# Reordering a linear-attention and channel-mix kernel: earlier loads of batches 1 and 2, and batch 3's gate input on GpSimd

## The chip, the cores and the metric

One core of a Trainium2 chip runs the whole program. The metric is device time in microseconds, taken over whole executions; the profile comes from one further execution. The engines are named as in the profile: PE is TensorE (PEld its weight loads), DVE is VectorE, ACT is ScalarE, POOL is GpSimd, and SP issues most of the DMAs.

## The reference

Two layers in a row, for 4 batches of 1088 positions. The first is attention with a polynomial sketch, 4 heads of 32:

```
phi(x) = outer(S1 x, S2 x)              # 8 x 8 = 64 features per position
kv = sum over s of phi(k) v^T           # 64 x 32 per head
z  = sum over s of phi(k)
x  = (phi(q) kv) / (phi(q) z + 1e-6)    # heads side by side: 128 per position
```

The second is a channel mix on x, with the position before it:

```
xk = mu_k x + (1 - mu_k) x_prev ;  xr = mu_r x + (1 - mu_r) x_prev
v  = relu(xk w_k)^2 w_v                 # 128 -> 1024 -> 128
out = sigmoid(xr w_r) * v
```

The output is 4 x 1088 x 128 in float32.

## The kernel before, in words

Everything fits on the chip at once. The positions of a batch are cut into 32 stretches of U = 34 units; with 4 heads that makes 128 partitions, so a batch of k or q is one [128, 34*32] tile. The kernel is written as small functions, each of which issues the instructions of one task, and one string, `ORDER`, lists all tasks in the order in which they are issued. Each engine works through its own tasks strictly in the order of the string; semaphores make it wait for what a task reads or overwrites. An entry such as `kp.2.0.G^an.1.2.V@...` is task kp of batch 2, half 0, on GpSimd (A is ScalarE, V VectorE, P VectorE with one operand from PSUM), tied behind the VectorE task an.1.2 by an added wait; the digits behind @ are the PSUM banks. There are 8 banks of 512 float32 columns.

The tasks of one batch b of the attention, in the order of their data:

- `turn.k`, `turn.q` (lines 261, 264): VectorE transposes k and q in blocks of 32. Batches in `WHOLE_K` are transposed in two instructions, so that four units lie side by side.
- `kproj` (274 or 280): S1 k and S2 k on TensorE into PSUM, in two halves. With the batch in `WHOLE_K` a half is 4 or 5 matmuls of 128 columns (line 274), otherwise four times as many on tiles of 32 columns (line 280). `abev` copies the halves to SBUF.
- `kp` (298): the outer products, phi(k), in two halves, on GpSimd or VectorE. `kvmm` (327) sums phi(k) v^T on TensorE, `kvev`, `kvt`, `kvtev` copy and transpose it.
- `zmm` (307), `zev`, `wmm` (315), `wsq` (318): z, folded with S into a small matrix SQ.
- `abw` (365, 369, 381, 386): S1 q, S2 q and q's product with z, on TensorE; `abwev` evacuates. `pw`, `den` (413, 414), `an` (422): the denominator, its reciprocal, and one factor divided by it. `qp` (431): the outer products phi(q).
- `qd` (440) or, for batch 0, `qt`, `qtt`: phi(q) transposed, on VectorE or TensorE. `xmm` (513, 496), `xt`, `xev`, `xtev`, `xs`: x on TensorE and its evacuation, with a shift for x_prev. `TURN = "ODDD"` says that batch 0 goes by TensorE and the others by VectorE; `WHOLE_Q` is read only where TURN is "O".

The channel mix works in nine groups g: two of 512 columns for each batch (g = 2b, 2b+1) and one, g = 8, of 256 for the last two units of all batches. `xk` (529) and `xkt` mix for w_k, `xh` and `xht` copy x in bf16 for the gate. Then per group, in four pieces: `f1` (553) = w_k times xk, `relu` (561) on ScalarE, `sq` (574, 576) on any engine, `f2` (586) into one bank. `rr` (599) is the gate's matmul, `sig` (607) the sigmoid, `fin` (612) the product, `st` (622, 618) the stores, two halves for each group. `cset` prepares small constants; `wset` converts the weights to bf16 (0 is w_k, 1 is w_v, 2 is w_r). `zz` (175) are matmuls on zeros into an otherwise free place.

The loads are issued ahead of all that, as `LOADS` lists them: S1 and S2, mu, k, q and v of each batch, weights w0 (w_k), w1 (w_v), w2 (w_r). All but three small ones go through SP's queue. A DMA's semaphore is used again by the eighth DMA after it, so that SP issues a load only when the one eight before it has landed.

Of the kernel before, what the change touches and what calls it, by code (L numbers as in the profile page):

```python
# [50 lines left out]
qp.2.0.V sq.3.1.V xh.1.0.G^sq.3.1.V kvev.2.V qp.2.1.G abwev.3.1.V kvev.3.V kvt.2 relu.3.2.A f1.3.0@45 relu.3.0.A
pw.3.2.G qd.2.0.V qd.2.1.V f1.3.3@01 relu.3.3.A kvtev.2.V sq.3.0.V f2.1.0@2 f2.1.1 kvt.3 kvtev.3.A f1.2.3@34
relu.2.3.A sq.2.3.V xh.1.1.G f2.1.2 den.3.2 f1.2.2@01 relu.2.2.A f2.1.3 sq.3.2.A xmm.2.2@3456 xev.2.0.A
sq.2.1.G^sq.2.3.V xt.2@0 fin.1 st.1.0.S st.1.1.S rr.2@1 xtev.2.V xs.2.G xh.2.0.G an.3.2.G f2.3.0@7 xev.2.1.V sq.2.2.A
sig.2.A xk.2.0 xkt.2 xk.2.1 qp.3.0.V f2.2.0@2 qd.3.0.V f2.3.1 f2.2.1 f1.4.0@01 f2.2.2 f1.4.1@34 sq.3.3.A relu.4.0.A
f2.2.3 fin.2 st.2.0.S st.2.1.S relu.4.1.A f1.4.3@56 relu.4.3.A qp.3.1.G^qp.3.0.V sq.4.0.G rr.3@0 sig.3.A f1.5.3@34
f2.3.2 f2.3.3 f1.4.2@56 qd.3.1.V relu.5.3.A fin.3 st.3.0.S st.3.1.S sq.4.3.V relu.4.2.A sq.4.2.V f1.5.0@12 sq.4.1.V
rr.4@0 sig.4.A xt.3@3 xh.2.1.V xtev.3.A sq.5.3.V xs.3.V relu.5.0.A sq.5.0.G^xs.3.V xmm.3.2@4567 f2.4.0@0 xev.3.0.A
xev.3.1.A xkt.3 f1.5.1@12 f2.4.1 f2.4.2 xk.3.0 xk.3.1 rr.5@3 xht.3.V relu.5.1.A sig.5.A f1.5.2@12 sq.5.1.V f2.4.3
xh.3.0.V relu.5.2.A sq.5.2.V f1.6.3@45 relu.6.3.A fin.4 st.4.0.S st.4.1.S xh.3.1.V f2.5.0@3 f1.6.0@67 f2.5.1 sq.6.3.V  # L60
# [13 lines left out]
def kernel(  # L74
# [51 lines left out]
    UH = {"k": {"": (0, U), "0": (0, 18), "1": (18, U)}, "q": {"": (0, U), "0": (0, 16), "1": (16, U)}}  # L126

    def load(what, eng):
        e = nc.sync if eng == "S" else nc.scalar if eng == "A" else nc.gpsimd
        x, b, i = what[0], int(what[1]), what[2:]  # L130
        if x == "S":
            e.dma_start(S16[R * b:R * b + R, :], S2 if b else S1)
        elif x == "m":
            e.dma_start(mu_row[b:b + 1, :], (moe_mu_r if b else moe_mu_k).rearrange("d -> () d"))
        elif x in "kq":
            src = (k if x == "k" else q)[b].rearrange("h (a u) d -> (h a) (u d)", u=U)
            lo, hi = UH[x][i]
            for lo, hi in ((lo, hi),) if i else ((0, U // 2), (U // 2, U)):
                e.dma_start((kin if x == "k" else qin)[b][:, lo * D:hi * D], src[:, lo * D:hi * D])
# [17 lines left out]
    nc.vector.memset(warm[:], 0.0)  # L157
# [94 lines left out]
    def turn(x, b, y, eng="V"):  # L252
        lo, hi = UH[x][str(y) if y < 2 else ""]
        t, src = (kT, kin) if x == "k" else (qT, qin)
        t = t[b % 2][:].rearrange("p u a -> p (u a)")
        if x == "k" and b in WHOLE_K:

            for c in (0, 2):
                u, n = CU[c]
                if lo <= u < hi:  # L260
                    nc.vector.transpose(_ap(t, [[32, 2], [P, n], [1, 32]], 32 * c),
                                        src[b][:, D * u:D * (u + 2 * n)].rearrange("p (c m d) -> p c m d", c=2, m=n))
        else:
            nc.vector.transpose(t[:, 32 * lo:32 * hi], src[b][:, D * lo:D * hi])  # L264
# [3 lines left out]
    def kproj(b, j, banks):  # L268
# [3 lines left out]
        for m in range(m0, m1):  # L272
            if b in WHOLE_K:
                nc.tensor.matmul(_ap(o[:, 32 * (m - m0):], [[n, 2], [1, 32]]),  # L274
# [402 lines left out]
```

## Time and profile before

| | us |
|---|---|
| median of 3 runs | 81.2 (81.06 to 81.69) |
| the profiled execution | 81.55 |
| its span, first to last instruction | 79.8 |
| first f1 matmul starts | 22.8 |
| last TensorE work ends | 75.35 |

The span is cut by the profile into windows, groups of like instructions and a chain of waits, the sequence of work that ended last. A row of a group gives line, engine, operation, tiles out<-in, shape, count, then busy us, the mean ns of one, and the idle time of the engine just before with what ended it. A row of the timeline begins with start and duration in us; a row of the chain likewise, with what the chain spent that stretch on. Neighbouring instructions of a kind are merged into one row (x16 is 16 of them). A TensorE matmul's own duration holds its latency, so that for TensorE the chain's pieces tell more than the means.

### The profile page before, as it was taken

How to read it: one execution, taken by the hardware profiler on the slowest of the kernel's cores; microseconds unless marked ns; L12 is line 12 of the kernel's file. 1: busy time of each engine (PE TensorE's matmuls, PEld its weight loads, DVE VectorE, ACT ScalarE, POOL GpSimd, SP SyncE). 2: the span in 40 equal slices, each digit the busy share in tenths (PEclk: the TensorE clock that was granted, in tenths of full speed). 3: DMA queues.
4: the chain of work that ended last, by engine and by line, in shares of the span. 5: the costliest groups of instructions: out<-in, count | busy, mean ns of one | idle time of the engine just before them, and what ended most of it. 6: DMA issues, size and time to landing. Idle time of an engine off the chain costs nothing.

```text
span 79.8 us, 3602 instructions
## 1 busy us (share of the span) xinstructions
PE 73.0 (91%) x1558; PEld 54.1 (68%) x1558; DVE 64.0 (80%) x121; ACT 58.5 (73%) x87; POOL 43.2 (54%) x55
## 2 busy tenths in 40 slices
...
GB/s 1 268 281 227 253 360 341 192 227 314 397 403 248 205 151 83 8 0 8 0 105 36 11 0 0 8 133 11 5 136 126 4 0 72 125 74 0 80 246 7
DMA packets 9876, 10.26 MB, mean 129 GB/s; under 512 B 1122, under 2 KB 7268, under 8 KB 9860
## 3 DMA queue, kind: packets, MB, share of 16 engines
...
q0 software_dynamic: 64, 0.13, 0.7%
q10 hardware_dynamic: 308, 0.13, 0.6%
...
HBM read 7.80 MB, written 2.23 MB: 126 GB/s over the span
## 4 chain that ended last, share of the span: by engine, by line
PE 83%; DMA 7%; issue 2%; SPq 1%; DVE 1%; DVEq 0%
PE ps L586 19%; PE ps L553 19%; DMA qx<-in_q_dram 7%; PE ps L327 6%; PE ps L513 6%; PE ps L386 5%; PE ps L599 5%; PE ps L274 5%; PE ps L175 3%; PE ps L369 2%; PE ps L451 2%; PE ps L479 1%; PE ps L307 1%; PE ps L496 1%; PE ps L280 1%
## 5 line engine op out<-in xcount | busy, mean ns | idle before, releaser
L561 ACT ACTIVATE k<-ps 128x1024 bf16<-128x1024 f32 (+1 forms) x36 | 33.3, 1010 | 0.6 <-PE ps L553 0.6
L586 PEld LDWEIGHTS <-k 128*128 128x128 bf16 x272 | 16.9, 98 | 4.1 <-issue 0.4
L586 PE MATMUL ps<-wv,k 128*128 128x128 bf16 x272 | 19.1, 219 | 0.0
L553 PE MATMUL ps<-xk,wk 128*128 128x512 bf16 x64 | 17.6, 379 | 0.0
L576 DVE TENSOR_TENSOR k<-k 128x1024 bf16<-128x1024 bf16 (+1 forms) x23 | 14.2, 648 | 0.9 <-ACT k L561 0.9
L431 POOL TENSOR_TENSOR qp<-an,abw 128x1024 f32<-128x1024 f32 (+1 forms) x5 | 10.2, 2047 | 1.7 <-DVE qp L431 1.7
L298 POOL TENSOR_TENSOR kp<-ab 128x1024 f32<-128x1024 f32 (+1 forms) x5 | 10.6, 2134 | 0.0
L576 POOL TENSOR_TENSOR k<-k 128x1024 bf16<-128x1024 bf16 x4 | 7.6, 1893 | 5.3 <-DVE qx L204 3.0
L574 ACT ACTIVATE k<-k 128x1024 bf16<-128x1024 bf16 x9 | 9.6, 1073 | 0.0
L175 PE MATMUL ps<-zero 128*128 128x512 bf16 x22 | 8.1, 489 | 1.0 <-DVE warm L157 1.0
L553 PEld LDWEIGHTS <-wk 128*128 128x128 bf16 x72 | 6.0, 100 | 2.6 <-DVE XT L532 0.3
L440 DVE STREAM_TRANSPOSE qpT<-qp 128x1152 f32<-128x1152 f32 (+1 forms) x6 | 7.6, 1294 | 0.1
L264 DVE STREAM_TRANSPOSE qT<-qx 128x1088 f32<-128x1088 f32 (+2 forms) x5 | 5.3, 1068 | 1.9 <-DMA qx<-in_q_dram 1.9
L622 POOL DMA_DIRECT2D out_dram<-k x2 | 1.3, 663 | 9.8 <-DVE k L612 9.8
L202 ACT COPY ab<-ps 128x320 f32<-128x320 f32 (+1 forms) x5 | 2.1, 419 | 5.5 <-PE ps L280 2.9
L529 DVE SCALAR_TENSOR_TENSOR xk<-ps,rat,qx 128x512 bf16<-128x512 f32 x8 | 5.7, 746 | 0.5 <-ACT qx L202 0.5
L607 ACT ACTIVATE k<-ps 128x512 f32<-128x512 f32 x8 | 5.2, 644 | 0.6 <-PE ps L599 0.6
L612 DVE TENSOR_TENSOR k<-ps,k 128x512 f32<-128x512 f32 x8 | 5.3, 668 | 0.1
L513 PE MATMUL ps<-qpT,kvt 32*32 32x256 f32 x192 | 5.2, 385 | 0.1
L327 PEld LDWEIGHTS ps<-kp,v 128*32 128x32 f32 x288 | 4.3, 110 | 1.3 <-issue 0.4
L327 PE MATMUL ps<-kp,v 128*32 128x64 f32 x288 | 4.9, 220 | 0.1
L386 PE MATMUL ps<-SQ,qT 128*32 128x96 f32 x192 | 5.0, 247 | 0.0
...
## 6 DMA issues: line engine op xcount, KB each, us to landing
out_dram<-k SPq DMA_DIRECT2D x28, 64.0 KB, 1.7
k<-in_k_dram SPq DMA_DIRECT2D x6, 272.0 KB, 6.9
qx<-in_q_dram SPq DMA_DIRECT2D x6, 272.0 KB, 6.3
...
```

The lines of the kernel that those rows point to most:

```text
L175: nc.tensor.matmul(PS[:, banks[0], :], zero[:], _ap(zero[:], [[0, 4], [1, P]]), skip_group_check=True)
L298: e.tensor_mul(o[:], _ap(a_, list(a_.ap[1:]) + [[0, R]]), _ap(b_, [list(b_.ap[1]), [0, R], list(b_.ap[2])]))
L327: nc.tensor.matmul(o[32 * h:32 * h + 32, :], vin[b][:, h, m, :], sb["kp", b, j][:, 4 * (m - KG[j][0]) + h].rearrange("p i j -> p (i j)"), ...
L386: nc.tensor.matmul(d, qT[b % 2][:, 16 * g + (quad(t) + c if TURN[b] == "O" else 4 * c + t), :], SQ[b][:], skip_group_check=True, tile_posi ...
L431: e.tensor_mul(o[:, :s1 - s0], _ap(a_, list(a_.ap[1:]) + [[0, R]]), _ap(b_, [list(b_.ap[1]), [0, R], list(b_.ap[2])]))
L440: nc.vector.transpose(sb["qpT", b][:].rearrange("p s y a -> p (s y a)")[:, F * s0:F * s1], sb["qp", b, g][:].rearrange("p s i j -> p (s i ...
L513: nc.tensor.matmul(o[32 * h:32 * h + 32, c, :], sb["kvt", b][y, f, 32 * h:32 * h + 32], m, start=(f == 0), stop=(f == 1), skip_group_check ...
L553: nc.tensor.matmul(h[:, c, :], wk[:, 2 * cp + c].rearrange("p y f -> p (y f)"), x, skip_group_check=True)
L561: nc.scalar.activation(o[:, :, :size(g)], h, RELU)
L574: nc.scalar.activation(o[:, :, :n], k1[:, :, :n], SQUARE)
L576: (nc.gpsimd if eng == "G" else nc.vector).tensor_mul(o[:, :, :n], k1[:, :, :n], k1[:, :, :n])
L586: nc.tensor.matmul(o[:, i * P:i * P + P], k2[:, c, i * P:i * P + P], wv[:, 2 * cp + c, :], start=(cp == 0 and c == 0 and i == 0), stop=(cp ...
```

## The change

- `WHOLE_K` gets batch 3. `WHOLE_Q` loses batches 1 and 2.
- `LOADS`: the two halves of k1 go ahead of v0; k2 and q2 go ahead of v1, w2 and w1. The halves now have names of their own ("a" and "b", 17 units each) and are cut where they were cut before.
- Loads of v on ScalarE's queue, were there any, would be issued behind the first activation. There are none.
- `ORDER` is another order of the same tasks. zz goes from 17 matmuls in the string to 9 (5 further ones ahead of the string stay). Among the tasks that change engine: abev.0.0 from VectorE to ScalarE, cset.4 from GpSimd to ScalarE, kp.0.1, kp.1.0 and kp.2.0 from VectorE to GpSimd, kp.3.0 the other way, qp.0.0 and qp.1.0 from GpSimd to VectorE, qp.2.0 and qp.3.0 the other way; sq on VectorE 0.1, 1.2, 1.3, 2.0, 2.1, 2.2, 3.2, 5.0 in place of 1.0, 1.1, 2.3, 3.0, 3.1, 8.3; xh.3.0 and xh.3.1 from VectorE to GpSimd; the last store, st.8.0, from SP to ScalarE, and st.6.0 from SP to GpSimd in place of st.6.1. New ties: kp.1.0 behind an.0.0, kp.2.0 behind an.1.2, wset.0 behind cset.3, and some others.

```diff
-WHOLE_K = (1, 2)
-WHOLE_Q = (0, 1, 2)
+WHOLE_K = (1, 2, 3)
+WHOLE_Q = (0,)
 LOADS = """
-S0@A S1@S m0@A m1@A k00@S k01@S q01@S q00@S v00@S v01@S v02@S v03@S k1@S q1@S w0@S v10@S v11@S v12@S v13@S w2@S w1@S
-k2@S q2@S k3@S q3@S v20@S v21@S v22@S v23@S v30@S v31@S v32@S v33@S
+S0@A S1@S m0@A m1@A k00@S k01@S q01@S q00@S k1a@S k1b@S v00@S v01@S v02@S v03@S q1a@S q1b@S w0@S k2a@S k2b@S q2a@S
+q2b@S v10@S v11@S v12@S v13@S w2@S w1@S k3a@S k3b@S q3a@S q3b@S v20@S v21@S v22@S v23@S v30@S v31@S v32@S v33@S
 """
 ORDER = """
-turn.k.0.0.V smm.0@0 cset.0 turn.k.0.1.V zz.5@7 kproj.0.1@0 abev.0.1.A kproj.0.0@1 turn.q.0.1.V cset.4.G abev.0.0.V
-smm.1@2 cset.1.V cset.2.G turn.q.0.0.V kp.0.0.G zz.1@7 zmm.0@3 zev.0.A zz.2@7 wmm.0 wsq.0 kp.0.1.P zz.2@7 abw.0.0@2
-abwev.0.0.A pw.0.0.P den.0.0 an.0.0.V abw.0.1@3 abwev.0.1.A pw.0.1.G^an.0.0.V kvmm.0@2 kvev.0.A zz.2@7 kvt.0
-turn.k.1.2.V zz.3@7 kproj.1.1@0 den.0.1 qp.0.0.G an.0.1.G qp.0.1.P abev.1.1.A kp.1.1.G kproj.1.0@1 abev.1.0.A
-kvtev.0.A qt.0.0@45 qtev.0.0.A turn.q.1.2.V wset.0.G qtt.0@2 qt.0.1@67 qttev.0.A zmm.1@3 zev.1.A qtev.0.1.A zz.2@5
-wmm.1 xmm.0.0@45 xt.0 xtev.0.A xev.0.0.A xmm.0.1@67 kp.1.0.P xev.0.1.A wsq.1 abw.1.1@3 cset.3 xs.0.V xk.0.0 xh.0.0.A
-xk.0.1 xh.0.1.A abw.1.0@1 abwev.1.1.V xkt.0 abwev.1.0.A f1.0.3@45 wset.2.G^xs.0.V relu.0.3.A f1.0.0@67 wset.1.G
-relu.0.0.A pw.1.2.G f1.1.3@23 f1.1.2@01 rr.0@4 sig.0.A relu.1.2.A relu.1.3.A turn.k.2.2.V kproj.2.1@5 den.1.2
-kproj.2.0@6 abev.2.0.A turn.q.2.2.V f1.1.0@01 kvmm.1@4 abev.2.1.V zmm.2@2 turn.k.3.2.V kproj.3.0@3 kp.2.0.P
-kproj.3.1@5 relu.1.0.A zev.2.A wmm.2 f1.0.1@01 sq.0.0.A kvev.1.A kvt.1 abev.3.1.V abev.3.0.A sq.0.3.G relu.0.1.A wsq.2
-f1.0.2@67 relu.0.2.A abw.2.0@3 an.1.2.G qp.1.0.G qp.1.1.G kvtev.1.A rr.1@0 qd.1.0.V qd.1.1.V sig.1.A sq.0.1.A
-abwev.2.0.V abw.2.1@1 abwev.2.1.A xmm.1.2@4567 turn.q.3.2.V kp.3.1.G zmm.3@3 xt.1@1 xev.1.1.V sq.0.2.A xtev.1.V
-kp.3.0.G zev.3.V f2.0.0@0 f2.0.1 xev.1.0.A wmm.3 xs.1.G sq.1.2.A f2.0.2 sq.1.3.A xkt.1 f2.0.3 xk.1.0 pw.2.2.G xk.1.1
...
-st.5.1.S sq.6.1.V sq.6.2.V f1.7.0@01 relu.7.0.A sq.7.0.V f2.6.0@2 xht.1.V sq.7.1.V f1.8.0@45 relu.8.0.A rr.7@3 f2.6.1
-f1.7.3@67 relu.7.3.A sq.7.3.V sq.8.0.V f2.6.2 f1.7.2@01 relu.7.2.A f2.6.3 sq.7.2.V f1.8.1@45 relu.8.1.A rr.6@6 sig.6.A
-f2.7.0@7 f1.8.3@01 relu.8.3.A f2.7.1 sq.8.1.V f1.8.2@45 relu.8.2.A f2.7.2 sig.7.A f2.7.3 xht.2.G rr.8@0 fin.6 st.6.0.S
-st.6.1.G sq.8.3.V sig.8.A sq.8.2.V f2.8.0@4 f2.8.1 fin.7 st.7.0.S st.7.1.A f2.8.2 f2.8.3 fin.8 st.8.0.S
+smm.0@0 turn.k.0.0.V cset.0 turn.k.0.1.V zz.5@7 kproj.0.0@0 turn.q.0.1.V abev.0.0.A kproj.0.1@1 kp.0.0.G abev.0.1.A
+kp.0.1.G smm.1@2 cset.1.V cset.4.A zmm.0@1 zev.0.A zz.2@7 wmm.0 wsq.0 zz.2@7 abw.0.1@2 abwev.0.1.A turn.q.0.0.V
+abw.0.0@1 abwev.0.0.A turn.k.1.2.V kproj.1.0@0 abev.1.0.A kvmm.0@3 kvev.0.A kproj.1.1@0 abev.1.1.A cset.2.G pw.0.1.P
+den.0.1 an.0.1.G pw.0.0.P den.0.0 an.0.0.V qp.0.0.P qp.0.1.P qtt.0@4 qttev.0.V kvt.0 kvtev.0.V qt.0.0@56 qtev.0.0.A
+zmm.1@0 zev.1.A turn.q.1.2.V qt.0.1@12 wmm.1 wsq.1 cset.3 xt.0 turn.k.2.2.V qtev.0.1.A kp.1.0.G^an.0.0.V xmm.0.0@56
+xev.0.0.A xtev.0.A xs.0.A xk.0.0 xh.0.0.A kp.1.1.G abw.1.1@0 xmm.0.1@12 xev.0.1.A abwev.1.1.A xkt.0 turn.q.2.2.V
+abw.1.0@3 abwev.1.0.A wset.0.G^cset.3 pw.1.2.G xk.0.1 f1.0.0@56 wset.2.G kproj.2.1@4 relu.0.0.A kproj.2.0@0 abev.2.1.A
+f1.1.0@45 den.1.2 xh.0.1.G an.1.2.V f1.0.2@67 sq.0.0.A abev.2.0.A zmm.2@0 relu.1.0.A kp.2.0.G^an.1.2.V zev.2.A
+qp.1.0.P kvmm.1@1 kvev.1.V f1.0.1@45 qp.1.1.G turn.k.3.2.V wmm.2 relu.0.2.A relu.0.1.A f1.0.3@23 relu.0.3.A kvt.1
+kvtev.1.A rr.0@6 f1.1.1@45 relu.1.1.A kproj.3.1@7 abev.3.1.A qd.1.0.V wsq.2 f1.1.2@23 relu.1.2.A sq.0.2.A abw.2.1@0
+abwev.2.1.A qd.1.1.V abw.2.0@7 kp.2.1.G turn.q.3.2.V abwev.2.0.V sq.0.1.V sq.0.3.A wset.1.G xmm.1.2@1234 xev.1.1.A
+pw.2.2.V xev.1.0.A xt.1@0 xtev.1.V den.2.2 xkt.1 kproj.3.0@7 abev.3.0.A sig.0.A sq.1.0.A xs.1.G^pw.2.2.V xk.1.0 xk.1.1
+kvmm.2@5 zmm.3@0 sq.1.1.A zev.3.V sq.1.2.V f2.0.0@6 f1.2.0@12 relu.2.0.A f2.0.1 kp.3.1.G an.2.2.V qp.2.0.G^an.2.2.V
+xh.1.0.G f1.2.3@34 f2.0.2 kp.3.0.P wmm.3 wsq.3 relu.2.3.A sq.2.3.A f2.0.3 f1.1.3@12 relu.1.3.A qp.2.1.G f2.1.0@0
+abw.3.1@3 abw.3.0@4 fin.0 qd.2.0.V kvev.2.A st.0.1.S abwev.3.1.A f1.2.1@67 relu.2.1.A abwev.3.0.V sq.2.0.V qd.2.1.V
+sq.1.3.V kvt.2 kvtev.2.A sq.2.1.V f1.2.2@12 relu.2.2.A f1.3.0@34 relu.3.0.A sq.2.2.V st.0.0.S f2.1.1 f1.3.1@67 f2.1.2
+rr.1@5 sig.1.A pw.3.2.G^sq.2.0.V den.3.2 xh.1.1.G^sq.2.2.V f2.1.3 fin.1 st.1.0.S an.3.2.G relu.3.1.A xmm.2.2@1234
+xev.2.1.A xt.2@5 f1.3.2@67 xtev.2.V xs.2.A kvmm.3@0 xev.2.0.V xk.2.0 qp.3.0.G qp.3.1.G xkt.2 relu.3.2.A f1.3.3@67
...
+sq.4.1.V sq.5.3.V sq.6.3.V f2.5.0@6 f1.7.2@45 f2.5.1 sq.4.2.V relu.7.2.A sq.6.0.V f1.6.2@01 relu.6.2.A xht.1.V f2.5.2
+sq.6.2.V f1.4.3@23 relu.4.3.A st.2.1.S f2.4.0@7 xh.2.1.G sq.7.2.V f2.5.3 f1.7.0@45 sq.4.3.V f2.4.1 relu.7.0.A
+f1.6.1@01 xht.2.V sq.7.0.V f2.4.2 relu.6.1.A sq.6.1.V st.3.1.S rr.4@2 sig.4.A f1.7.1@34 relu.7.1.A f2.6.0@5 f2.4.3
+rr.5@2 sig.5.A f2.6.1 f1.7.3@01 f1.8.1@34 xh.3.0.G relu.7.3.A f2.6.2 rr.6@2 f2.6.3 fin.4 st.4.0.S f1.8.0@01 fin.5
+st.5.0.S sq.7.1.V relu.8.1.A sig.6.A st.5.1.S sq.7.3.V f1.8.2@67 relu.8.2.A relu.8.0.A fin.6 st.6.1.S sq.8.0.V
+f2.7.0@3 xh.3.1.G^sq.6.1.V rr.7@4 f2.7.1 f1.8.3@67 f2.7.2 f2.7.3 sq.8.1.V f2.8.0@5 st.4.1.S sig.7.A rr.8@4 relu.8.3.A
+sq.8.3.A sq.8.2.V sig.8.A fin.7 st.7.1.A st.7.0.S st.6.0.G f2.8.1 f2.8.2 f2.8.3 fin.8 st.8.0.A
 """
...
-            for lo, hi in ((lo, hi),) if i else ((0, U // 2), (U // 2, U)):
-                e.dma_start((kin if x == "k" else qin)[b][:, lo * D:hi * D], src[:, lo * D:hi * D])
+            e.dma_start((kin if x == "k" else qin)[b][:, lo * D:hi * D], src[:, lo * D:hi * D])
...
-    for entry in LOADS.split():
-        load(*entry.split("@"))
-    nc.scalar.activation(warm[:], warm[:], SIGMOID)
+
+    for late in (0, 1):
+        for entry in LOADS.split():
+            if late == (entry[0] == "v" and entry.endswith("A")):
+                load(*entry.split("@"))
+        if not late:
+            nc.scalar.activation(warm[:], warm[:], SIGMOID)
```

More of the change, by code (lines that the diff above doesn't have):

```diff
@@ L46 @@
-f1.0.2@67 relu.0.2.A abw.2.0@3 an.1.2.G qp.1.0.G qp.1.1.G kvtev.1.A rr.1@0 qd.1.0.V qd.1.1.V sig.1.A sq.0.1.A
-abwev.2.0.V abw.2.1@1 abwev.2.1.A xmm.1.2@4567 turn.q.3.2.V kp.3.1.G zmm.3@3 xt.1@1 xev.1.1.V sq.0.2.A xtev.1.V
-kp.3.0.G zev.3.V f2.0.0@0 f2.0.1 xev.1.0.A wmm.3 xs.1.G sq.1.2.A f2.0.2 sq.1.3.A xkt.1 f2.0.3 xk.1.0 pw.2.2.G xk.1.1
-f1.1.1@12 relu.1.1.A f1.2.0@45 relu.2.0.A wsq.3 fin.0 st.0.0.S st.0.1.S f1.3.1@67 den.2.2 sq.1.1.V an.2.2.V abw.3.0@0
-abw.3.1@1 relu.3.1.A f1.3.2@23 f1.2.1@45 sq.2.0.A sq.1.0.V relu.2.1.A xht.0.G kp.2.1.G kvmm.2@6 kvmm.3@7 abwev.3.0.A
@@ L51 @@
[L51 to L60, printed above, removed]
@@ L61 @@
-relu.6.0.A f1.6.1@12 relu.6.1.A f2.5.2 f1.6.2@45 relu.6.2.A f2.5.3 f1.7.1@67 relu.7.1.A sq.6.0.V fin.5 st.5.0.S
-st.5.1.S sq.6.1.V sq.6.2.V f1.7.0@01 relu.7.0.A sq.7.0.V f2.6.0@2 xht.1.V sq.7.1.V f1.8.0@45 relu.8.0.A rr.7@3 f2.6.1
-f1.7.3@67 relu.7.3.A sq.7.3.V sq.8.0.V f2.6.2 f1.7.2@01 relu.7.2.A f2.6.3 sq.7.2.V f1.8.1@45 relu.8.1.A rr.6@6 sig.6.A
-f2.7.0@7 f1.8.3@01 relu.8.3.A f2.7.1 sq.8.1.V f1.8.2@45 relu.8.2.A f2.7.2 sig.7.A f2.7.3 xht.2.G rr.8@0 fin.6 st.6.0.S
-st.6.1.G sq.8.3.V sig.8.A sq.8.2.V f2.8.0@4 f2.8.1 fin.7 st.7.0.S st.7.1.A f2.8.2 f2.8.3 fin.8 st.8.0.S
+smm.0@0 turn.k.0.0.V cset.0 turn.k.0.1.V zz.5@7 kproj.0.0@0 turn.q.0.1.V abev.0.0.A kproj.0.1@1 kp.0.0.G abev.0.1.A
```

8 lines of the change are left out of this document (7 added, 1 removed).

## The prediction

> **What bounds the kernel now.** I read the page's head and its chain first, then busy time before and after the first f1 matmul, then the chain piece by piece, then the timeline of the first 22 us.
>
> ```profile
> span 79.8 us, 3602 instructions
> PE 73.0 (91%) x1558; PEld 54.1 (68%) x1558; DVE 64.0 (80%) x121; ACT 58.5 (73%) x87; POOL 43.2 (54%) x55
> PE 83%; DMA 7%; issue 2%; SPq 1%; DVE 1%; DVEq 0%
> PE ps L586 19%; PE ps L553 19%; DMA qx<-in_q_dram 7%; PE ps L327 6%; PE ps L513 6%; PE ps L386 5%; PE ps L599 5%; PE ps L274 5%; PE ps L175 3%; PE ps L369 2%; PE ps L451 2%; PE ps L479 1%; PE ps L307 1%; PE ps L496 1%; PE ps L280 1%
> core 0: us, PE busy (x) PEld busy (x) DVE busy (x) ACT busy (x) POOL busy (x), PEclk, DMA share, GB/s
> 8.70:22.86 14.16, 14.05 (x300) 11.12 (x301) 10.75 (x23) 6.76 (x16) 11.56 (x12) 1.00 1.06 306
> 22.86:75.40 52.54, 52.26 (x1164) 39.94 (x1164) 48.60 (x84) 49.91 (x69) 29.64 (x26) 1.00 0.26 69
> ```
>
> The chain is 83% TensorE. From 22.86 us, where the first f1 begins, to 75.40 TensorE is busy 52.26 of 52.54 us: 0.28 us of idle time is all that a better order could fill there, with ScalarE (49.91) close behind. That stretch can start earlier or hold less TensorE work, and little else. Ahead of it TensorE looks busy too, but the chain's 3% on L175, 2.4 us, are the zz matmuls, filler that computes nothing. So the first stage has slack, and its length is set on VectorE and GpSimd.
>
> ```profile
> 2.07 5.41 DMA qx<-in_q_dram
> 14.45 0.65 PE ps L175 x3
> 22.86 1.84 PE ps L553 x8
> 25.14 2.02 PE ps L274 x18
> 28.86 1.04 PE ps L280 x70
> 75.44 0.42 DVE rt L612
> ```
>
> **Part 1: an earlier zmm.0.**
>
> ```profile
> 5.58 1.23 PE L280 MATMUL ps<-SK,kT 128*32 128x64 f32 x72
> 8.20 0.45 DVE L204 COPY ab<-ps 128x320 f32<-128x320 f32 x1
> 8.71 0.38 PE L307 MATMUL ps<-ab 128*32 128x32 f32 x18 [1.04 <-DVE ab L204]
> L204 POOL COPY SQ<-SK 128x64 f32<-128x64 f32 x4 | 0.8, 233 | 3.2 <-DVE SK L215 3.2
> ```
>
> Before, abev.0.0 stands behind turn.q.0.1 on VectorE, which waits for q01 until 7.48 (2.07 + 5.41), so zmm.0 starts at 8.71. After, both evacuations are ScalarE's, behind a kproj.0 that ends at 6.81: done near 7.3, and zmm.0 goes at 7.4. It does not carry through: wmm.0 needs cset.1, which stays behind turn.q.0.1, and cset.4's four copies now stand ahead of zev.0 on ScalarE (0.8 us, by what GpSimd took). Worth by itself: nothing, because of part 2.
>
> **Part 2: k1 ahead of v0, and a new VectorE order.**
>
> ```profile
> 8.84 0.33 SPq L139 DMA_DIRECT2D qx<-in_q_dram  x1
> k<-in_k_dram SPq DMA_DIRECT2D x6, 272.0 KB, 6.9
> GB/s 1 268 281 227 253 360 341 192 227 314 397 403 248 205 151 83 8 0 8 0 105 36 11 0 0 8 133 11 5 136 126 4 0 72 125 74 0 80 246 7
> 12.12 0.31 DVE L406 TENSOR_TENSOR pw<-abw,ps 128x144 f32<-128x144 f32 x1 [0.99 <-ACT abw L202]
> 13.19 0.31 DVE L422 TENSOR_TENSOR an<-abw,den 128x144 f32<-128x144 f32 x1
> 13.41 1.36 DVE L261 STREAM_TRANSPOSE kT<-k 128x576 f32<-128x576 f32 x2
> 18.51 2.18 POOL L210 TENSOR_SCALAR wk<-wk_f,omu 128x1024 bf16<-128x1024 f32 x1
> L431 DVE TENSOR_TENSOR qp<-an,abw 128x1152 f32<-128x1152 f32 x2 | 2.7, 1349 | 0.0
> L264 DVE STREAM_TRANSPOSE qT<-qx 128x1088 f32<-128x1088 f32 x3 | 3.8, 1283 | 0.0
> ```
>
> SP's issue of q1's second half at 8.84 had waited for q00 to land. k1 is then next: two transfers of 272 KB. At 253 to 360 GB/s (slices 8 to 12 us) 557 kB take 1.5 to 2.2 us, so k1 lands at 10.4 to 11.0; I take 10.7. kvmm.0 now stands behind kproj.1.0 and does not wait for v0, which lands 2 us after k1. But turn.k.1.2 stands in VectorE's queue ahead of all of batch 0's pw, den, an and qp, and they wait with it. From 10.7 VectorE runs in sequence: turn.k.1.2 1.36; pw, den and an twice (12.12 to 13.50 is 1.38 for one, the second sends its an to GpSimd: 2.4 together); qp.0.0 1.35 and qp.0.1 1.20 (by size); turn.q.1.2 1.28; four small ones, qttev, kvtev, wsq.1 and cset.3, 1.0 by the 0.31 of pw. That is 8.6 us, some 0.4 less where neighbours overlap: cset.3 is done at 18.9 to 19.3. wset.0 is tied to it and takes 2.18 on GpSimd, which has kp.1.0 and kp.1.1 until about then anyway. So the first f1 starts near 21.3; TensorE's own work (abw.1.0 last) and xk.0.0, behind turn.k.2.2, end at about the same time. I take 21.5 for 22.8: **-1.3 us**. Bounds: 21.0 with k1 at 10.4 and every overlap, 22.2 with k1 a microsecond late: -1.8 to -0.6. Four zz are left in this stage; the others cost no path time where a wait ended last anyway. From 10.7 on, v0, q1, w0, k2 and q2 are 2.7 MB, v1, w2 and w1 another 1.15 MB: at the 192 to 403 GB/s of the slices to 24 us k2 lands near 18, q2 near 20, w1 near 24, each ahead of its use in the new order (turn.k.2.2 from 19.1, kvmm.1, rr.0, f2.0.0): no wait.
>
> **Part 3: batch 3's keys become WHOLE_K.** kproj.3 changes from line 280 (36 matmuls on 32-column tiles) to line 274 (9 full ones). The rows above have both: 2.02 us for L274's 18 records, 1.04 to 1.23 for L280's 70 to 72. All of it lies in the stretch with no idle time: **+0.9 us** (+0.8 to +1.0). This speaks against the change. Its second transpose is 0.1 us of VectorE, under cover. WHOLE_Q without 1 and 2 does nothing (only batch 0 has TURN "O"), nor do the halves "a" and "b" (17 + 17 units as before) or the two-pass load loop (no v is on ScalarE).
>
> **Part 4: who does what.**
>
> ```profile
> L298 POOL TENSOR_TENSOR kp<-ab 128x1280 f32<-128x1280 f32 x2 | 4.8, 2398 | 0.0
> L298 DVE TENSOR_TENSOR kp<-ab,ps 128x1280 f32<-128x1280 f32 x2 | 2.9, 1449 | 0.0
> L204 POOL CAST x<-qx 128x544 bf16<-128x544 f32 x3 | 1.9, 638 | 3.9 <-DVE k L576 3.8
> L204 DVE CAST x<-qx 128x544 bf16<-128x544 f32 x3 | 1.4, 453 | 0.0
> ```
>
> kp: three go from VectorE to GpSimd, one comes back; sq: VectorE gets three more in balance, GpSimd two fewer; qp: two each way. Added up over all moved operations with their mean durations, VectorE is some 1.2 us lighter, ScalarE 0.8 heavier (all of it cset.4 and abev.0.0, in the idle first stage), GpSimd 0.9 lighter. None passes TensorE's 53.4 us: nothing on the path. xh.3.0 and xh.3.1 take 0.64 instead of 0.45 each on GpSimd, but rr.6 and rr.7, which read them, come many groups later, and GpSimd stood idle 3.8 us before one such cast: nothing; +0.2 each if that cover is gone.
>
> The Trainium skill's GPSIMD Engine Reference (section 3, Performance versus the Vector engine) calls VectorE roughly twice as fast for elementwise work and advises against GpSimd there; kp is 1.65 times apart here and the casts 1.4. By its factor kp.2.0 would be 0.5 us longer, which would use up the margin in case 3 below.
>
> **Part 5: TensorE's starved stretch.**
>
> ```profile
> 31.32 0.17 PE ps L381 x2
> 31.49 0.13 issue
> 31.63 0.34 PE ps L381 x10
> 31.97 0.67 PE ps L386 x25
> 33.19 0.80 PE ps L386 x32
> 40.07 0.26 PE ps L381 x14
> 40.33 1.34 PE ps L386 x64
> ```
>
> abw.2 takes 2.11 us here (the first five pieces) and abw.3 1.60 (the last two): 0.5 us lost around a wait for issue, soon after kproj.3's 72 short matmuls; I bound what else goes that way by as much again. With 54 pairs fewer some of it should go. Not shown, so -0.9 to +0.4; I take **-0.3**.
>
> **Part 6: the tail.**
>
> ```profile
> 75.34 0.87 ACTq L622 DMA_DIRECT2D out_dram<-k  x2
> 76.28 0.38 SPq L618 DMA_DIRECT2D out_dram<-rt  x1
> ```
>
> fin.8 ends at 75.86, but its store waits behind group 7's on SP until 76.28. After, it stands behind st.7.1 on ScalarE's queue, which is free near 76.1, since fin.7 comes one f2 piece (0.2) earlier: **-0.2** (0 to -0.4). st.6.0 on GpSimd is issued microseconds earlier: nothing.
>
> **Part 7: new waits.** A wholly new order, with ScalarE 93% busy beside TensorE: **+0.4** (0 to +1.5) over today's 0.28.
>
> **Sum.** -1.3 + 0.9 - 0.3 - 0.2 + 0.4 = -0.5 us. The profiled execution took 81.55 us (79.8 of span, 1.75 around it) and would take 81.05. It stands 0.35 over the median of the runs, 81.2, which becomes **80.7 us**.
>
> **The rivals.** About 1% (0.8 us) is what a measurement of this kernel can tell from no change.
>
> 1. Forecast, no change: 80.7, its own range 80.4 to 81.9. Chance 0.40.
>
> 2. Faster: k1 lands at 10.4 and the first f1 starts at 21.1 (-1.7), the starved stretch goes altogether (-0.9), the tail gives 0.2, kproj costs 0.9, new waits 0.3: -1.6, so 79.6. For it: the 2.4 us of filler, and VectorE's line of ready work. Against it: kproj.3 takes half back. Chance 0.38.
>
> 3. Slower, GpSimd sets xmm.1. kp.2.0 moves from VectorE (1.45) to GpSimd (2.40) and is tied to an.1.2; qp.1.1 stands behind it, qd.1.1 behind that, then xmm.1. On VectorE two transposes (2.6) and xk.0.0, xkt.0, xk.0.1, den.1.2 and an.1.2 (2.7, an estimate from pw and an by size) follow cset.3 at 19.1, so an.1.2 ends near 24.4; then kp.2.0 2.4, qp.1.1 2.0, and two transposes on VectorE 2.4: xmm.1 near 31.2. TensorE's work ahead of it is about 10.2 us (seven f1 at 0.46, kproj.2 2.0, half of kproj.3 0.9, abw.2 1.6, the rest 2.5), so it gets there at 31.7. The margin is 0.5; beyond it TensorE idles one for one. If VectorE's line is 2 us late, that is +1.5 on the forecast: 82.2. For it: VectorE was busy 10.75 of 14.16 us in the first stage and gets more there. Chance 0.14.
>
> 4. Slower, the clock.
>
> ```profile
> 0.99 2.31 PE L175 MATMUL ps<-zero 128*128 128x512 bf16 x5 [0.99 <-DVE warm L157]
> ```
>
> These five fillers took 0.46 us each, the three at 14.45 0.22: TensorE starts at half speed here. If it falls back in the thinner stretch from 11.5 to 16 us, some 3 us of matmuls take twice as long, half of that under VectorE's sequence: +1.5, 82.2. It decides only if TensorE stands idle long; I expect about 1 us at most, while it waits for turn.k.1.2 near 11.5. Chance 0.08. The page "TensorE: Matmul & The Clock Gate" of the Trainium skill (Part 1) puts the fall at an idle window of about 3.4 us; by that the clock stays up, and the 1.00 granted in both rows above agrees so far.
>
> Faster by over 1% 0.38, within 0.40, slower 0.22. The range 79.0 to 82.5 takes in cases 2 to 4 at their likely sizes with some 0.3 to 0.6 beyond, and leaves out the joint ends of the bounds.
>
> **What would show it.** Part 1: zmm.0 (L307) near 7.4. Part 2: batch 1's transposes (L261) at 10.7, the first L553 at 21.0 to 22.2; a start after 22.8 breaks the forecast. Part 3: 18 more L274 records and 0.9 us more of them and L280 on the chain. Part 4: TensorE never idle before rr.6 and rr.7. Part 5: abw.2 at 1.6 or 2.1 us. Part 6: the last store issued 0.2 us after fin.8. Part 7: idle time under 0.7 us from the first f1 on. Case 3: xmm.1 waiting for qpT. Case 4: a granted clock under 1.00.

## The result and the profile after

The changed kernel takes 79.72 us (median of 4 executions, 79.64 to 80.23), the kernel before 81.31 (81.06 to 81.69) beside it. The ratio is 0.986 with a 95% interval of 0.9814 to 0.9905. The forecast was 80.7, no change, with a range of 79.0 to 82.5. The time lies in that range, but what came is the second case, faster, which had been put at 79.6. Ratios here leave out executions more than 1.5% above the quickest of their kernel; where that leaves few of them, the median of all stands beside the ratio.

The profiled execution took 79.79 us (81.55 before). The head of its page, with busy time by engine, and the summary of the chain:

```profile
span 77.9 us, 3471 instructions
PE 71.4 (92%) x1486; PEld 55.3 (71%) x1496; DVE 63.7 (82%) x121; ACT 60.2 (77%) x94; POOL 42.3 (54%) x49
PE 82%; ACT 6%; DVE 5%; issue 2%; DVEq 0%
```

The transfer of q that held 7% of the chain of before is gone from it, and ScalarE has come in with 6%. The window view, cut at the first f1 and at the end of TensorE's work:

```profile
core 0: us, PE busy (x) PEld busy (x) DVE busy (x) ACT busy (x) POOL busy (x), PEclk, DMA share, GB/s
8.70:21.25 12.55, 12.03 (x270) 9.84 (x268) 11.23 (x24) 6.61 (x14) 10.23 (x9) 1.00 0.97 287
21.25:73.80 52.55, 51.64 (x1101) 41.73 (x1110) 47.85 (x81) 50.63 (x71) 29.30 (x26) 1.00 0.30 80
```

The first f1 starts at 21.25 instead of 22.79. From there to the end of TensorE's work it is as long as before, 52.50 against 52.55 us, though TensorE is busy 0.6 us less in it and idle 0.91 us instead of 0.28. What follows TensorE's end is 0.33 us shorter (4.09 against 4.42). So in this pair of profiles the whole difference of 1.9 us between the two spans lies ahead of the first f1 and behind the last matmul.

The chain of waits piece by piece (start, duration, what it was spent on):

```profile
11.32 1.09 PE ps L278 x10
12.41 1.14 PE ps L331 x72
...
19.64 0.25 PE ps L385 x11
19.89 0.45 issue
...
20.65 1.22 PE ps L390 x29
...
21.90 0.84 ACT k L565
...
29.58 0.80 PE ps L390 x32
...
31.20 1.37 PE ps L517 x58
```

From 0.99 to 21.9 us the chain is TensorE's own sequence, with only short waits for issue in it (the longest 0.45 us): no transfer and no VectorE work ended last there in this profile. In a second profile of the same kernel the chain leaves TensorE from 11.15 to 14.47 us for the evacuation of abw.0 and batch 0's pw, den, an and qp.0 on VectorE, so the two lines are close to a tie. From 21.9 to 26.4 the chain shown here passes through ScalarE's relu and evacuations. After that it is TensorE's again, but for 3 us from 46.2 (an evacuation of x, then xk) and 0.7 us at 52.9 (a fin). The rows of the timeline that answer to the steps of the prediction (start, duration, instruction, and in brackets the idle time before it with what ended it):

```profile
7.52 0.38 PE L311 MATMUL ps<-ab 128*32 128x32 f32 x18
8.88 1.13 PE L373 MATMUL ps<-SQ,qT 128*128 128x96 f32 x8
9.39 1.37 DVE L265 STREAM_TRANSPOSE kT<-k 128x576 f32<-128x576 f32 x2
17.91 0.16 DVE L230 TENSOR_TENSOR rat<-tmp,mu 128x1 f32<-128x1 f32 x1
18.23 2.18 POOL L214 TENSOR_SCALAR wk<-wk_f,omu 128x1024 bf16<-128x1024 f32 x1 [0.56 <-POOL kp L302]
24.54 2.40 POOL L302 TENSOR_TENSOR kp<-ab 128x1280 f32<-128x1280 f32 x1 [0.53 <-ACT ab L206]
29.09 1.22 DVE L444 STREAM_TRANSPOSE qpT<-qp 128x1024 f32<-128x1024 f32 x1
73.87 0.42 DVE L616 TENSOR_TENSOR rt<-ps,rt 128x256 f32<-128x256 f32 x1 [0.42 <-PE ps L590]
74.44 0.41 ACTq L622 DMA_DIRECT2D out_dram<-rt  x1
```

zmm.0 is at 7.52, batch 1's keys are transposed from 9.39 with no wait for their load, cset.3 ends at 18.07, and the last store is issued 0.15 us after fin.8.

### The profile page after: what moved, and what is told of

It is laid out like the page before. It is cut to its first block, busy times and chain, and to the rows that moved or that the text cites. A ratio compares the mean times of both kernels' runs of the same rounds, so it can differ in the third digit from the quotient of the medians.

```text
span 77.9 us, 3471 instructions
## 1 busy us (share of the span) xinstructions
PE 71.4 (92%) x1486; PEld 55.3 (71%) x1496; DVE 63.7 (82%) x121; ACT 60.2 (77%) x94; POOL 42.3 (54%) x49
## 4 chain that ended last, share of the span: by engine, by line
PE 82%; ACT 6%; DVE 5%; issue 2%; DVEq 0%
PE ps L590 20%; PE ps L557 14%; PE ps L179 7%; PE ps L390 6%; PE ps L278 6%; PE ps L517 6%; PE ps L603 5%; ACT k L565 3%; PE ps L331 3%; PE ps L373 3%; PE ps L455 2%; DVE xk L533 2%; PE ps L284 2%; PE ps L500 1%; ACT k L578 1%
## 5 line engine op out<-in xcount | busy, mean ns | idle before, releaser
L302 POOL TENSOR_TENSOR kp<-ab 128x1024 f32<-128x1024 f32 (+1 forms) x7 | 14.9, 2146 | 6.6 <-ACT ab L206 5.9
L557 PE MATMUL ps<-xk,wk 128*128 128x512 bf16 x54 | 16.1, 380 | 0.1
L208 POOL CAST x<-qx 128x544 bf16<-128x544 f32 x6 | 3.8, 638 | 10.5 <-DVE k L580 10.5
L578 ACT ACTIVATE k<-k 128x1024 bf16<-128x1024 bf16 (+1 forms) x9 | 9.1, 1024 | 0.1
L278 PEld LDWEIGHTS ps<-SK,kT 128*128 128x128 f32 x54 | 6.6, 192 | 0.7 <-issue 0.2
L278 PE MATMUL ps<-SK,kT 128*128 128x64 f32 x54 | 7.0, 275 | 0.1
L179 PE MATMUL ps<-zero 128*128 128x512 bf16 x14 | 5.8, 558 | 1.0 <-DVE warm L157 1.0
L206 ACT COPY abw<-ps 128x384 f32<-128x384 f32 (+1 forms) x6 | 3.0, 504 | 3.2 <-PE ps L373 1.9
L580 POOL TENSOR_TENSOR k<-k 128x1024 bf16<-128x1024 bf16 x2 | 3.8, 1892 | 2.3 <-DVE k L580 2.3
L603 PE MATMUL ps<-wr,x 128*128 128x128 bf16 x64 | 4.9, 219 | 0.2 <-DVE XT L536 0.2
```

Source lines behind the costliest of these rows:

```text
L179: nc.tensor.matmul(PS[:, banks[0], :], zero[:], _ap(zero[:], [[0, 4], [1, P]]), skip_group_check=True)
L302: e.tensor_mul(o[:], _ap(a_, list(a_.ap[1:]) + [[0, R]]), _ap(b_, [list(b_.ap[1]), [0, R], list(b_.ap[2])]))
L557: nc.tensor.matmul(h[:, c, :], wk[:, 2 * cp + c].rearrange("p y f -> p (y f)"), x, skip_group_check=True)
L578: nc.scalar.activation(o[:, :, :n], k1[:, :, :n], SQUARE)
L580: (nc.gpsimd if eng == "G" else nc.vector).tensor_mul(o[:, :, :n], k1[:, :, :n], k1[:, :, :n])
L603: nc.tensor.matmul(p[:, i * P:i * P + P], x, wr[:, y, :], start=(i == 0 and y == 0), stop=(y == 1), skip_group_check=True)
```

## The experiments

Two questions came first: whether batch 3's wide projection costs what its matmuls take, or pays for itself because short matmuls are followed by waits for issue; and whether the loads or the order of VectorE bring the earlier start of the first f1. No experiment leaves out a part of the computation: the fillers that some drop compute nothing. Where a time of the first f1 or of the end of TensorE's work is given, it is the row of that kernel's timeline.

**Batch 3's keys narrow again, in the changed kernel.**

```diff
-WHOLE_K = (1, 2, 3)
+WHOLE_K = (1, 2)
```

> The changed kernel with WHOLE_K = (1, 2) again, so that kproj.3 goes back to 72 short matmul pairs; order and loads stay as changed. Theory A (the wide form costs 0.9 to 1.0 us of TensorE and nothing else): 0.9 us faster than the changed kernel, about 78.8 us, ratio to before 0.970. Theory B (the 54 fewer pairs of the wide form are what took the waits for issue out of abw.2 and xmm.1): the waits for issue behind kproj.3 come back, 79.7 us, ratio 0.985, with abw.2 taking 2 us again.

Measured: ratio 0.9852 (0.9778 to 0.9927), but by two executions of ten; the median of all ten is 81.10, while the changed kernel's was 79.72 and 79.86 in its two sets. The chain of its profile, and the window from its first f1 on:

```profile
32.16 0.46 PE ps L284 x20
32.62 0.99 issue
33.61 0.53 PE ps L284 x20
...
36.09 0.50 PE ps L590 x6
36.59 0.84 issue
```

```profile
20.28:74.56 54.28, 51.42 (x1157) 40.86 (x1164) 48.48 (x81) 50.97 (x73) 29.32 (x26) 1.00 0.29 76
```

The narrow form saves only 0.2 us of TensorE work from the first f1 on (51.42 against 51.64) and adds 1.95 us of idle time (54.28 - 51.42 = 2.86 against 0.91), nearly all of it in two waits for issue, one between the short matmuls of kproj.3 and one in f2.0 soon behind them. But this profile is of an execution of 80.97 us, which the ratio leaves out, and no profile shows whether the two that it rests on (79.68 and 80.28) had these waits. That the wide form costs 0.9 us, so that this kernel would gain them, is out. In this order the wide form is worth between nothing and 1.7 us: the ratio supports the first, the trace the second, and the median of all ten lies at 1.2 to 1.4.

Waits for issue come and go. Neither profile of the kernel before has one of TensorE above 0.16 us, though its keys are narrow. The traces also hold the transfers on the instruction queue, 16 KB each (12 in this profile, 11 in the changed kernel's). In all fourteen profiles TensorE stands idle for issue twelve times for 0.18 us or more, and each of these waits ends 1.3 to 1.6 us after such a transfer has ended; here the transfers end at 32.11 and 35.94 us and the waits at 33.61 and 37.43. This points to the supply of instructions, of which short matmuls need more, but no run tests it.

**Batch 3's keys wide, in the kernel before.** The same edit the other way round: `WHOLE_K = (1, 2, 3)`.

> The kernel before with WHOLE_K = (1, 2, 3) and nothing else changed. Theory A (the wide form is pure cost): 0.9 us slower, 82.2 us, ratio 1.011, abw.2 still at 2.1 us. Theory B (fewer pairs, no wait for issue): kproj.3 costs 0.95 more and abw.2 and xmm.1 together give 0.9 back, 81.3 us, ratio 1.000.

Measured: 1.004 (0.9987 to 1.0094); the median of all ten executions, 81.35, is that of the kernel before beside it, 81.38. A cost of 0.9 us (1.011) is out. The chain of its profile:

```profile
28.11 2.15 PE ps L274 x18
...
31.54 0.26 PE ps L381 x14
...
33.83 1.43 PE ps L513 x61
35.26 0.30 PE ps L307 x18
```

The piece that follows xmm.1 in the chain of before:

```profile
35.98 0.31 PE ps L307 x18
```

kproj.3 costs 1.1 us more than before (2.15 against 1.04), and abw.2 with xmm.1 behind it takes 0.94 less: 3.72 us from 31.54 to 35.26 here, 4.66 before (31.32 to 35.98). Two more profiles with the old order and narrow keys, one of the kernel before and one with only its loads changed, take 4.38 and 4.86 for these pieces, so 0.7 to 1.1 us come back. In the first of the two there is hardly a wait for issue between the pieces (0.03 us): the pieces themselves are longer, abw.2 2.01 us against 1.74 here and xmm.1 1.82 against 1.43. From the first f1 to TensorE's end it takes 52.72 us here and 52.24 to 52.65 in the three profiles with narrow keys. So the gain in the starved stretch about pays for the matmuls.

**The new loads alone, in the kernel before.**

```diff
-... q00@S v00@S v01@S v02@S v03@S k1@S q1@S w0@S v10@S v11@S v12@S v13@S w2@S w1@S
-k2@S q2@S k3@S q3@S ...
+... q00@S k1@S v00@S v01@S v02@S v03@S q1@S w0@S k2@S q2@S
+v10@S v11@S v12@S v13@S w2@S w1@S k3@S q3@S ...
```

> The kernel before with the changed kernel's load order and nothing else. Theory C (the loads bring the first stage's gain: with k1's long rows behind q instead of v0's short ones, q01 lands near 6.0 us instead of 7.5, and all that waits for it moves up): first f1 1.0 to 1.4 us earlier, 80.2 us, ratio 0.986, perhaps 0.3 us less where wset.2 waits for w2. Theory D (the early landing of q01 is chance, or the old order waits for something else next, kp.0.0 on GpSimd or v0): 81.2 us, ratio 1.000.

Measured: 0.9985 (0.9929 to 1.0042). k1 landed at 9.68 us instead of 12.32, but its transpose stands where the old order has it on VectorE, and kvmm.0, which the old order puts ahead of kproj.1, waits for v0, now loaded behind k1:

```profile
12.10 0.31 DVE L422 TENSOR_TENSOR an<-abw,den 128x144 f32<-128x144 f32 x1
12.32 1.37 DVE L261 STREAM_TRANSPOSE kT<-k 128x576 f32<-128x576 f32 x2
12.00 1.21 PE L327 MATMUL ps<-kp,v 128*32 128x64 f32 x72 [0.66 <-DMA v<-in_v_dram]
```

The chain of this profile runs through that transfer of v. zmm.0 starts at 7.62, and the first f1 at 22.18. The loads alone bring nothing that shows.

**The old loads, in the changed kernel.** `LOADS` as before, with v0 ahead of k1 and v1, w2, w1 ahead of k2.

> The changed kernel with the old load order and nothing else. k1 then lands near 12.3 us, and turn.k.1.2, which stands ahead of batch 0's pw, den, an and qp on VectorE, starts 3 us later than in the changed kernel. Theory C (order and loads hang together): VectorE's line sets the first f1, which comes 1.5 to 2.5 us later, 81.5 us, ratio 1.003. Theory D (the order alone brings the gain): 79.9 us, ratio 0.987.

Measured: 1.0137 (1.0048 to 1.0226), slower than the kernel before, and more so than expected. The timeline of this kernel, then the same two TensorE instructions in the timeline of the changed kernel, then this kernel in windows of 2 us (columns as above):

```profile
11.27 1.37 DVE L265 STREAM_TRANSPOSE kT<-k 128x576 f32<-128x576 f32 x2 [1.54 <-DMA k<-in_k_dram]
12.70 1.79 PE L278 MATMUL ps<-SK,kT 128*128 128x64 f32 x10 [1.08 <-DVE kT L265]
14.41 2.15 PE L331 MATMUL ps<-kp,v 128*32 128x64 f32 x72
21.57 1.37 DVE L265 STREAM_TRANSPOSE kT<-k 128x576 f32<-128x576 f32 x2 [0.65 <-DMA k<-in_k_dram]
23.62 0.38 PE L557 MATMUL ps<-xk,wk 128*128 128x512 bf16 x1 [0.18 <-DVE xk L533]
```

```profile
11.16 1.25 PE L278 MATMUL ps<-SK,kT 128*128 128x64 f32 x10
12.34 1.21 PE L331 MATMUL ps<-kp,v 128*32 128x64 f32 x72
```

```profile
10.00:12.00 2.00, 1.61 (x15) 1.30 (x14) 0.73 (x2) 0.83 (x2) 1.92 (x2) 1.00 1.05 399
12.00:14.00 2.00, 1.30 (x9) 1.31 (x10) 1.83 (x7) 0.16 (x1) 0.78 (x3) 0.85 1.08 278
14.00:16.00 2.00, 2.00 (x63) 1.88 (x66) 1.90 (x5) 0.42 (x1) 1.05 (x2) 0.50 1.10 237
16.00:18.00 2.00, 2.00 (x36) 1.83 (x25) 1.31 (x3) 0.50 (x2) 1.42 (x1) 0.80 1.01 298
```

kproj.1.0 starts at 12.70 instead of 11.16, because its keys land late, and then the granted clock falls to 0.50: it takes 1.71 us from there to the start of kvmm.0 instead of 1.18, and kvmm.0 2.15 instead of 1.21. That makes 1.5 + 0.5 + 0.9 = 3.0 us (rounded) by the end of kvmm.0; 2.4 are left at the first f1, at 23.62. The mean granted clock was low in all four executions of this kernel, 0.958 to 0.979. k2, late as well, holds VectorE for 0.65 us there, but TensorE waits only 0.18 for what comes of it. So the new order needs the new loads, and case 4 of the prediction is a mechanism that this kernel has, though the changed kernel does not meet it.

**The changed kernel again**, as the control beside the next ones.

> The changed kernel itself, as the base of the runs beside it: ratio to before 0.986, first f1 at 21.0 to 21.5 us, from there to the end of TensorE's work 52.5 us.

Measured: 0.9858 (0.9791 to 0.9926), median 79.86. In its profile the first f1 starts at 21.05 and TensorE ends at 73.98.

**The kernel before again**, for a second profile of its first stage.

> The kernel before once more, for its trace. In its first profile q01 landed at 7.48 us; with the same loads in two other kernels it landed at 6.2. If 7.48 was one execution's, q01 lands near 6.2 here, zmm.0 starts near 7.9 and the first f1 near 22.0 us, so that the change's gain in the first stage is about 1.0 us and not the 1.5 that the first two profiles show. If it belongs to the kernel, 7.5 and 22.8 again.

Measured: 80.59 us, a span of 78.8. q01 landed at 5.88 here, not at 7.48, zmm.0 started at 8.08, and the first f1 at 22.16 instead of 22.79. The long transfer in the chain of the first profile was that execution's own.

**The fillers left out or halved.** The two zz.2 of `ORDER` are left out (twice, with two labels), or each cut to one matmul:

```diff
-... zev.0.A zz.2@7 wmm.0 wsq.0 zz.2@7 abw.0.1@2 ...
+... zev.0.A wmm.0 wsq.0 abw.0.1@2 ...
```

> The changed kernel without its last four fillers (the two zz.2 around wmm.0). Theory E (the fillers fill waits for zev.0 and wsq.0 and cost nothing): within 0.2 us of the changed kernel, ratio 0.986. Theory F (they hold the clock up; the run with the old loads showed the granted clock at 0.50 from 14 to 16 us after TensorE had waited 1.1 us): granted clock under 1.00 somewhere between 8 and 16 us and 0.5 to 1.5 us slower, ratio 0.995 to 1.005. Theory G (they are on the path): 0.9 us faster, 78.8 us, ratio 0.975.

> The changed kernel without its last four fillers a second time. Its first executions lay between 79.2 us, at a granted clock of 1.00, and 82.8, at a mean of 0.95. Theory F (the fillers hold the clock up): again some executions with a mean clock under 0.96, 2 us and more slower. Theory E (they only cost): all near 79.3 us, ratio 0.980, clocks of 0.98 and more.

> The changed kernel with one filler instead of two in both places. By the trace wmm.0 could start 0.2 us sooner, and abw.0 0.15: 0.3 us faster than the changed kernel, ratio 0.982, the clock held at 0.98 or more in every execution. If the clock needs all four: executions with a mean clock under 0.96.

Measured: the first set without them took 79.24, 79.81, 81.01 and 82.75 us, the last at a mean granted clock of 0.947; no ratio came of it. The second gave 0.9836 (0.9737 to 0.9935), between 78.81 and 82.02, with no clock under 0.992. With one matmul each, 0.9872 (0.9781 to 0.9962): five executions between 78.91 and 79.97 and one of 83.1 at a clock of 0.946. Without fillers the first f1 starts at 20.78 and 20.84 us, 0.2 to 0.5 earlier than in the two profiles of the changed kernel. That is a gain that these intervals can't tell from none, and two executions of sixteen lost about 3 us at a clock of 0.95. That the missing fillers caused those two is not shown: in most executions the clock held, and kernels with all their fillers have executions at a low clock too (104.53 us at 0.671, of the kernel before; 103.45 at 0.672, with the casts of the next experiment on VectorE).

**xh.3.0 and xh.3.1 back on VectorE**, at the place of xh.3.0, run twice.

```diff
-... f1.8.1@34 xh.3.0.G relu.7.3.A ...
+... f1.8.1@34 xh.3.0.V xh.3.1.V relu.7.3.A ...
-f2.7.0@3 xh.3.1.G^sq.6.1.V rr.7@4 ...
+f2.7.0@3 rr.7@4 ...
```

> The changed kernel with xh.3.0 and xh.3.1 on VectorE again, both where xh.3.0 stands in the order. By part 4 of the prediction the move to GpSimd was worth nothing: ratio 0.986, within 0.3 us. If VectorE is the bound near the end, its 0.9 us of added work shows there: up to 0.9 us slower, ratio 0.997.

> The kernel with xh.3.0 and xh.3.1 on VectorE a second time. In its first trace the time from the first f2 to the last was 37.08 us, to 0.01 us that of the changed kernel, and k1 had landed 1.7 us later. Theory H (the move costs nothing, and late landings made the first run slow): ratio 0.986, within 0.4%. Theory I (it costs): 0.995 again.

Measured: 0.9954 (0.9895 to 1.0014) and 0.9924 (0.9837 to 1.001). From the first to the last f2 both traces have 37.08 us, as the changed kernel has: the casts cost nothing on VectorE and nothing on GpSimd. But after TensorE's end they take 4.46 and 4.52 us instead of 4.09. The waits on SP's queue (waiting line, what for, us in total, times, longest), in the second of these kernels:

```profile
SPq L676 <- PEq L676: 1.1, 2, 0.5
```

and in the control:

```profile
SPq L676 <- PEq L676: 0.6, 2, 0.5
```

It is the end of the program, where SP waits for TensorE's sequencer, that is longer. Why is open, and the casts may have no part in it: with batch 3's keys narrow and with batch 1's, both with the casts on GpSimd, what follows TensorE's end takes 4.55 and 4.65 us. In the first of the two traces TensorE also waited 1.26 us for the transposed keys of batch 1, since k1 landed only at 10.83 there, and the first f1 was at 21.62; in the second k1 landed at 9.21, and the first f1 was at 20.84. The place of the casts, far behind, is no reason for that landing. The granted clock held through that wait (columns as above):

```profile
10.00:12.00 2.00, 1.09 (x10) 0.93 (x8) 1.07 (x2) 0.81 (x2) 1.83 (x4) 1.00 1.08 255
12.00:14.00 2.00, 1.65 (x38) 1.58 (x42) 1.78 (x7) 0.28 (x1) 0.41 (x2) 1.00 1.04 371
```

The two ratios lie 0.5 to 0.8 us above the changed kernel's. How much of that is a real loss can't be settled: both intervals reach below 0.99.

**Batch 1's keys narrow, in the changed kernel.** `WHOLE_K = (2, 3)`.

> The changed kernel with WHOLE_K = (2, 3): kproj.1, in the first stage, goes to 72 short matmul pairs and 1.0 us less of TensorE. Theory A (short form is cheaper wherever it stands): first f1 0.7 to 1.0 us earlier, 78.9 us, ratio 0.976. Theory B (108 more instructions in that stretch make TensorE wait for issue, as the short kproj.3 did with 1.0 and 0.8 us): waits for issue of 0.5 us or more between kproj.1 and the first f1, which then comes at 21.0 or later, 79.7 us, ratio 0.986.

Measured: 1.0049 (0.9996 to 1.0102), where the changed kernel beside it had 0.9858. The first f1 starts early, at 20.43, but the chain then has waits for issue that the changed kernel lacks at these places:

```profile
23.92 0.25 PE ps L311 x13
24.16 0.35 issue
...
32.46 0.17 PE ps L483 x5
32.63 0.37 issue
```

From the first f1 to TensorE's end it needs 53.85 us, 1.35 more: TensorE is busy 0.62 longer (52.26 us) and idle 0.68 longer. The short matmuls that it adds lie at 11 to 14 us, and these waits come 10 and 20 us later, so the link from one to the other is argued and not shown.

## Where the prediction was right and where it failed, step by step

The sign was right and the time lies in the range, but the forecast was no change. Two terms were wrong: part 1, put at nothing, and part 5, put at -0.3.

Three profiles with the old first stage and five with the new one bound how far a single one can be trusted. The first f1 starts at 22.79, 22.16 and 22.00 us with the old one (both profiles of before, and the one with batch 3's keys wide), mean 22.3, and at 21.25, 21.05, 20.28, 21.62 and 20.84 with the new one (the changed kernel twice, batch 3's keys narrow, and the casts on VectorE twice), mean 21.0.

**Part 1 was right on the start and wrong on its worth.** zmm.0 came at 7.52 (7.4 forecast), and abw.0 at 8.88. "Worth by itself: nothing" does not hold. With the old first stage zmm.0 starts at 8.71, 8.08 and 7.92, and each time the first f1 follows it by 14.08 us (14.56 with the new loads alone, where kvmm.0 waits 0.66 for v0). The rows of zmm.0 in the last two:

```profile
8.08 0.38 PE L307 MATMUL ps<-ab 128*32 128x32 f32 x18
7.92 0.38 PE L307 MATMUL ps<-ab 128*32 128x32 f32 x18
```

With the new one zmm.0 starts at 7.52, 7.33, 7.29, 7.29 and 7.26, and the first f1 follows by 13.73, 13.72, 12.99, 14.33 and 13.58. Both chains of the changed kernel pass through zmm.0. By the means 0.9 of the 1.3 us are zmm.0's earlier start, or 0.7 without the first profile of before, whose q01 landed late; 0.4 us are what lies behind it.

**Part 2 had the right size by luck.** The means give -1.3 us, the forecast's value, but most of it is part 1's. VectorE's line from turn.k.1.2 to cset.3 took 8.7 us (8.6 forecast). But k1 landed at 9.29, not at 10.7 (8.6 to 10.8 over the runs with the new loads), so the wait for turn.k.1.2 that was to come near 11.5 did not come: VectorE's pw.0.0 then waits 0.28 us for the evacuation of abw.0, which follows zmm.0, and no more for k1. Where k1 did land as forecast, at 10.83 in the first trace with the casts on VectorE, TensorE waited 1.26 us and the first f1 came at 21.62, near the 21.5 forecast. That loads and order bring the earlier start only together was not said in the prediction; the two experiments on the loads show it. The chain behind zmm.0 holds 2.70 us of filler before and 0.97 after. No run puts the missing fillers back, so their share of the gain is open.

**Parts 3 and 5 together failed.** Part 3's +0.9 was right as a price: kproj.3 cost 1.1 us more in the kernel before. Part 5, "I take -0.3", was the mis-sized term: abw.2 and xmm.1 gave back 0.94 in the kernel before (0.7 to 1.1 over three profiles), about the lower bound that the prediction had named. It read 0.5 us off abw.2 alone and took less than that; in the pair of profiles shown abw.2 gave back 0.38 and xmm.1, which it had not priced, 0.56. In the changed order abw.2 took 1.62 us (29.58 to 31.20), and 2.01 with batch 3's keys narrow. The two parts come to +0.2 in the kernel before, and in the changed one to a gain if the median of the first experiment is taken, where +0.6 was forecast. "This speaks against the change" was not borne out.

**Part 4 was right** for the stretch it spoke of: nothing waits for the moved casts, and TensorE idles nowhere before rr.6 and rr.7 on their account. Its balance of the engines was off: VectorE is 0.3 us lighter over the span (1.2 forecast) and ScalarE 1.7 heavier (0.8 forecast), 0.7 of it from the first f1 on and not in the first stage (49.91 to 50.63).

**Part 6 was right** in sign and nearly in size: the last store is issued 0.15 us after fin.8 instead of 0.42, and the span behind TensorE's end is 0.33 shorter (0.2 forecast).

**Part 7 stays undecided.** Idle time from the first f1 on rose by 0.63 us in the first pair of profiles (0.28 to 0.91) and by 0.39 in the second (0.70 to 1.09), where 0.4 was forecast; both totals pass the 0.7 named as the limit. No TensorE task moved across the first f1. TensorE's busy time behind it fell by 0.6 us in the first pair (52.26 to 51.64) and rose by 0.3 in the second (51.54 to 51.84), where parts 3 and 5 gave +0.6. Together the three parts, forecast at +1.0, came to -0.05 in the first pair, to +0.7 in the second, and to +0.3 by the means (52.50 and 52.93 against 52.55 and 52.24).

The sum was -0.5 with the forecast's terms. With the measured ones it is -1.3 + 0.3 - 0.3 = -1.3, where the medians fell by 1.6; the remaining 0.3 is within what the profiles of one kernel differ by (81.55 and 80.59 us for the two of before).

**Case 2** came, and with it two of its own terms: its first f1 at 21.1 (21.25 and 21.05), and the starved stretch that gives back 0.9. Its reason for the first is not what brought it: k1 landed even earlier than it asked (9.29 and 8.74 against 10.4), but the first f1 hung on zmm.0. **Case 3** did not come: an.1.2 ended at 24.3 and kp.2.0 at 26.94, as worked out, and the transpose ahead of xmm.1 at 30.31, while TensorE reached xmm.1 at 31.20. The margin was 0.9 us (0.5 forecast). **Case 4** did not come either: the granted clock is 1.00 in both windows. With the old loads it did fall, after a wait of the length that the prediction took for harmless (1.08 us), but it held through 1.26 us in another profile. So the length of that wait alone does not decide it, and what does is open.
